# Reordering one core's attention and feed-forward kernel: value products, transposes, PSUM banks and the last tile

## The chip, the cores and the metric

The kernel runs on one core of a Trainium2 chip. The metric is the device time of one launch in microseconds (us). A core has TensorE (PE in the profile, with its weight loads as PEld), VectorE (DVE), ScalarE (ACT), GpSimd (POOL) and SyncE (SP). In this kernel POOL issues most of the loads.

## The reference, cut to what matters

```python
scores = q @ k.T / 8 + bias                   # 8 batches, 8 heads, 576 positions, head size 64
attn   = softmax(scores)
x      = (attn @ v).transpose(0, 2, 1, 3).reshape(4608, 512)
out    = ((x @ w_a) * (x @ w_b)) @ w_out      # 512 -> 1536 -> 512, bilinear, no activation
```

The kernel treats heads in pairs: 32 pairs, four for each batch. The 576 positions of a head are four tiles of 128 and a "tail" of 64.

## The kernel before

Step `s` computes the scores and exponentials of pair `s` and the value products of pair `s - 1`. Between them it puts **units**: pieces of the feed-forward part of earlier batches, four matmuls of 512 columns each. A unit is either `ff_a` (then a copy on ScalarE), `ff_b` (then a product on VectorE) or a third of an output tile.

The kernel takes eight banks of PSUM, the memory that matmuls write to, and its pools divide them so: `ps_sc` two buffers of two banks for scores, `ps_ff` two for the units ("ffn"), `ps_av` one and `ps_tr` one. From pair 12 on the units also take `ps_tr` at every third turn. The two pools with one bank:

```python
def t_k(p, where):                  # key transposes of pair p: four tiles, two tails
    ps = bank(where, BF16, f"trk{p}")
    for t in range(NM):
        nc.tensor.transpose(ps[:, 128 * t:128 * t + 128], blocks(kn, p)[:, t, :, :], ident)
    ...                             # c_k copies the bank to KT on VectorE, which frees it

def qk_tail(p):                     # scores with a tail; the last product has its own bank
    ...
    pt = bank(TR if p < R3 else AV, FP32, f"qktt{p}")      # R3 = 12

def norm(p, j0):                    # reciprocal of the sums and multiply, both read the bank
    ...

XD = set(range(11, NP - 1))         # pairs whose result is transposed by DMA, not on PE
```

One step, before the change. `A` are value products in bank `AV` (tiles 0 to 2) and in `TR` or, from step 12 on, `AV` (tiles 3 and 4). `N` is their normalisation, `U` a place for units, `e` says that pair `s + 1` is one of the first twelve:

```python
steps += [lambda: qk(s, 0), lambda: ex(s, 0), U, lambda: ex(s, 1), A(0, 1, 2), N(0), U,
          lambda: mul(s, 0), A(3, 4), N(3)]
if s - 1 in XD:
    steps += [lambda: t_x(s - 1), lambda: turns(s)]
steps += [U, lambda: mul(s, 1)]
if e:
    steps += [lambda: t_q(s + 1, TR), lambda: c_q(s + 1)]
steps += [lambda: qk(s, 2), lambda: ex(s, 2), U, lambda: ex(s, 3)]
if e:
    steps += [lambda: t_k(s + 1, TR), lambda: c_k(s + 1)]
steps += [U, lambda: mul(s, 2), U, lambda: mul(s, 3),
          lambda: qk_tail(s), lambda: ex_tail(s), U]
...
```

Steps 5 to 8 have fewer units than places (7, 6, 4 and 4), later steps have 9. The last output tile is computed in two halves of 256 columns, so that the first can be copied while the second is computed:

```python
def ff_last(c, tt):
    po = ff_bank(f"po{c}_{tt}")
    for x, cols in enumerate((slice(0, 256), slice(256, 512))):
        ...                                              # 12 matmuls into po[:, cols]
        copy(None if x else nc.scalar, ob[:, cols], po[:, cols])
        ...
```

The softmax here doesn't subtract the row's maximum and nothing guards it: scores larger than these inputs give would overflow.

## Time and profile before

| | kernel before |
|---|---|
| time | 425.61 us, median of 3 runs (425.33 to 426.5) |
| span of the profiled run | 423.3 us |
| PE / ACT / DVE busy | 97% / 58% / 47% |
| matmuls, and weight loads | 3420 each |

TensorE's share and its slices are shown in the prediction below, with the waits. Two rows of the page complete them: the granted TensorE clock and the busy share of the DMA engines, in tenths, in 40 slices of 10.6 us.

```profile
PEclk9999999999999999999999999999999999999999
DMA  9999999995929940999099908731021002002004
```

The clock is full nearly everywhere, so distances between matmuls can be compared nearly across the whole run. (Not so at the very start: up to 9.0 us fp32 transposes stand 213 ns apart and afterwards 109, which the first digit of the row doesn't show.) The DMA engines are full for the first nine slices, to about 95 us.

### The profile page before, as it was taken

To read this page: it belongs to the slowest core of one execution; us is meant where nothing else is said; L and a number is where in the kernel's file an instruction comes from. 1 tells how busy PE (TensorE), PEld (TensorE's weight loads), DVE (VectorE), ACT (ScalarE), POOL (GpSimd) and SP (SyncE) were. 2 spreads that over 40 slices of the span, in tenths; PEclk is the share of its full clock that TensorE was granted. 3 is DMA by queue.
4 is the path that set the end of the run, shared out by engine and by line. 5 is a ranking of instruction groups with operands and counts; after the bars stand their busy time and mean duration, and the time that the engine had idled before them with its cause. 6 is when DMAs were issued, how large, how long until landed. Compare 5 with 4: busy or idle time off the path is not lost.

```text
span 423.3 us, 8500 instructions
## 1 busy us (share of the span) xinstructions
PE 411.6 (97%) x3420; PEld 204.6 (48%) x3420; DVE 199.4 (47%) x491; ACT 243.9 (58%) x345; POOL 119.4 (28%) x161
## 2 busy tenths in 40 slices
PE   8899999999999999999999999999999999999995
PEld 3574555555444444444444444444444454444443
DVE  3775566555642565245535553355425650331420
ACT  4986566756656666576656665666556642322321
POOL 9999829704437000820083003000000000000000
PEclk9999999999999999999999999999999999999999
DMA  9999999995929940999099908731021002002004
GB/s 161 184 175 174 160 171 158 167 184 38 88 27 172 175 58 15 139 180 125 16 96 197 137 16 60 168 70 33 15 88 33 9 17 99 2 0 101 0 1 101
DMA packets 163017, 40.33 MB, mean 95 GB/s; under 512 B 153401, under 2 KB 158305, under 8 KB 162977
## 3 DMA queue, kind: packets, MB, share of 16 engines
q0 software_dynamic: 110448, 18.75, 60.3%
q1 hardware_dynamic: 51248, 20.59, 25.1%
q10 hardware_dynamic: 1280, 0.43, 0.5%
q8 instruction: 27, 0.44, 0.4%
q14 instruction: 14, 0.11, 0.1%
HBM read 38.77 MB, written 9.45 MB: 114 GB/s over the span
## 4 chain that ended last, share of the span: by engine, by line
PE 89%; DMA 5%; ACT 2%; DVE 1%; issue 1%; ACTq 0%; POOL 0%; DVEq 0%; POOLq 0%
PE pa L511 21%; PE pb L511 21%; PE po L542 21%; PE av L412 8%; PE qk L342 8%; DMA qn<-in_q_dram 3%; PE av L403 3%; PE qkt L367 2%; PE qkt L370 1%; ACT at L353 1%; DMA vm<-in_v_dram 1%; DMA k<-in_k_dram 1%; PE trx L475 1%; PE po L530 1%; DVE XG L449 1%
## 5 line engine op out<-in xcount | busy, mean ns | idle before, releaser
L353 ACT ACTIVATE at<-qk 128x1024 bf16<-128x1024 f32 x128 | 126.4, 1023 | 24.3 <-PE qk L342 24.1
L523 DVE TENSOR_TENSOR g<-pb,ha 128x512 bf16<-128x512 f32 x108 | 74.7, 692 | 118.0 <-PE pb L511 98.7
L511 PE MATMUL pa<-xn,wa 128*128 128x512 bf16 x432 | 111.2, 379 | 0.5 <-ACT ha L518 0.5
L511 PE MATMUL pb<-xn,wb 128*128 128x512 bf16 x432 | 111.2, 379 | 0.0
L518 ACT ACTIVATE ha<-pa 128x512 f32<-128x512 f32 x108 | 64.5, 598 | 69.8 <-PE pa L511 69.8
L542 PE MATMUL po<-wo,g 128*128 128x512 bf16 x420 | 100.2, 379 | 0.0
L361 DVE TENSOR_TENSOR at<-at,W 128x512 bf16<-128x512 bf16 (+1 forms) x128 | 60.1, 484 | 10.3 <-ACT at L353 8.8
L511 PEld LDWEIGHTS <-wa 128*128 128x128 bf16 x432 | 38.9, 98 | 48.5 <-issue 9.3
L511 PEld LDWEIGHTS <-wb 128*128 128x128 bf16 x432 | 38.9, 98 | 46.3 <-issue 6.6
L546 ACT ACTIVATE ob<-po 128x512 f32<-128x512 f32 x35 | 20.9, 597 | 67.9 <-PE po L542 67.9
L542 PEld LDWEIGHTS <-g 128*128 128x128 bf16 x420 | 37.2, 98 | 44.0 <-issue 7.4
L123 POOL DMA_DIRECT2D vm<-in_v_dram x32 | 28.2, 929 | 102.5 <-PE av L412 101.7
L412 PE MATMUL av<-vm,at 128*128 128x65 bf16 x992 | 43.3, 193 | 0.0
L412 PEld LDWEIGHTS <-at 128*128 128x128 bf16 x992 | 39.5, 97 | 3.9
L448 DVE RECIPROCAL rc<-av 128x6 f32<-128x6 f32 x64 | 12.1, 188 | 55.9 <-PE av L412 53.6
L403 PE MATMUL av<-vt,att 128*128 128x130 bf16 x156 | 34.9, 224 | 0.4
L381 ACT ACTIVATE att<-qkt 128x1024 bf16<-128x1024 f32 x32 | 32.6, 1020 | 0.0
L449 DVE TENSOR_TENSOR XG<-av,rc 128x384 bf16<-128x384 f32 x64 | 31.4, 491 | 2.2
L123 POOL DMA_DIRECT2D qn<-in_q_dram x28 | 24.4, 926 | 26.5 <-PE trq L291 19.1
L123 POOL DMA_DIRECT2D kn<-in_k_dram x28 | 24.5, 920 | 5.5 <-DMA vm<-in_v_dram 2.5
L342 PE MATMUL qk<-QTb,KTb 64*128 64x512 bf16 x160 | 24.2, 381 | 0.0
L403 PEld LDWEIGHTS <-att 128*128 128x128 bf16 x156 | 15.3, 98 | 15.3 <-DVE XG L449 10.7
(121 smaller groups left out, 247.0 us busy)
## 6 DMA issues: line engine op xcount, KB each, us to landing
out_dram<-ob SPq DMA_DIRECT2D x32, 256.0 KB, 3.8
vm<-in_v_dram POOLq DMA_DIRECT2D x28, 128.0 KB, 5.3
qn<-in_q_dram POOLq DMA_DIRECT2D x24, 128.0 KB, 8.4
kn<-in_k_dram POOLq DMA_DIRECT2D x24, 128.0 KB, 8.5
wa<-in_moe_w_a_dram POOLq DMA_DIRECT2D x3, 512.0 KB, 6.8
wb<-in_moe_w_b_dram POOLq DMA_DIRECT2D x3, 512.0 KB, 9.2
wo<-in_moe_w_out_dram POOLq DMA_DIRECT2D x1, 1536.0 KB, 13.4
W<-bias_tab POOLq DMA_DIRECT2D x4, 192.0 KB, 5.0
```

The source lines that it names most:

```text
L123: nc.gpsimd.dma_start(out=(vm[b % 2][:, h0:h1, t, 0:Dh] if dst is None else dst[b % 2][:, :].rearrange("p (t h d) -> p t h d", h=H, t=NM)[ ...
L342: nc.tensor.matmul(out=ps[:, hh, :], lhsT=kT_(p, t)[r, :], rhs=qT[r, :, :], start=True, stop=True)
L353: nc.scalar.activation(out=at[:, :, :], in_=ps[:, :, :], func=ACTF.Exp, scale=scale)
L361: nc.vector.tensor_tensor(out=at[:, :, lo:hi], in0=at[:, :, lo:hi], in1=w[:, :, y:(None if z < 0 else z):-1], op=MULT)
L381: nc.scalar.activation(out=at[:, 0:1024].rearrange("p (a x) -> p a x", a=2), in_=ps[:, :, :], func=ACTF.Exp, scale=scale)
L403: nc.tensor.matmul(out=pav[:, slot, :, :], lhsT=x, rhs=vt[b // 2 % 2][:, 4 * i + hp, :, 0:Dh + 1], start=fresh, stop=True, skip_group_chec ...
L412: nc.tensor.matmul(out=pav[:, slot, hh, :], lhsT=x, rhs=vm[i][:, 2 * hp + hh, t, 0:Dh + 1], start=False, stop=True, skip_group_check=True)
L449: nc.vector.tensor_tensor(out=xg[:, j0:j0 + n, :, :], in0=pav[:, 0:n, :, 0:Dh], in1=rc.unsqueeze(3).to_broadcast([128, n, 2, Dh]), op=MULT)
L511: nc.tensor.matmul(out=ff[key][:, :], lhsT=w[df // FW][:, mc, 128 * (df % FW):128 * (df % FW) + 128], rhs=xn_sb[mc][:, xin(c)], start=(i = ...
L518: nc.scalar.activation(out=ha[:, :], in_=ff["pa"][:, :], func=ACTF.Copy)
L523: nc.vector.tensor_tensor(out=g_sb[df][:, :], in0=ff["pb"][:, :], in1=ff["ha"][:, :], op=MULT)
L542: nc.tensor.matmul(out=po[:, :], lhsT=g_sb[df][:, 128 * tt:128 * tt + 128], rhs=wo_sb[:, df, :], start=(df == 0), stop=(df == NDF - 1))
```

## The change

Its intent is to close waits of TensorE for a PSUM bank, and to take a few transposes off it. The diff, cut to its core (left out: the DMA transposes of pair `s - 1` move along with the half in part 1):

```diff
-    warm_up(1)                                  # part 6
+    warm_up(3)
-    XD = set(range(11, NP - 1))                 # part 2
+    XD = set(range(8, NP - 1))
 def ff_last(c, tt):                             # part 5
-        po = ff_bank(f"po{c}_{tt}")
         for x, cols in enumerate((slice(0, 256), slice(256, 512))):
+            po = ff_bank(f"po{c}_{tt}_{x}")
@@ around step 4: part 4 (pair 4 behind the first two units)
-    t_k(4, FF)      # and c_k(4, ACT): now behind av_part(3, 3)
-    qk1(4, 0)
-    ex(4, 0)
-    qk1(4, 1)
-    ex(4, 1)
     norm(3, 0)
     norm(3, 3)
+    ff_mm(0, 0, wa_sb, "pa", 0, 3)
     t_x(3, AV, range(3))
-    ff_mm(0, 0, wa_sb, "pa", 0, 3)
-            steps += [U, U, lambda: qk1(4, 2), lambda: ex(4, 2), U, ...
+            steps += [U, U, lambda: qk1(4, 0), lambda: ex(4, 0), lambda: qk1(4, 1), U, lambda: ex(4, 1),
+                      lambda: qk1(4, 2), U, lambda: ex(4, 2), lambda: qk1(4, 3), lambda: ex(4, 3),
@@ steps 5 to 31
-                      lambda: mul(s, 0), A(3, 4), N(3)]
+                      lambda: mul(s, 0)]
+            av34 = [A(3, 4), N(3)]              # part 1: from step 12 on one unit later
+            if s < R3:
+                steps += av34
             steps += [U, lambda: mul(s, 1)]
+            if s >= R3:
+                steps += av34
+            steps += [lambda: qk(s, 2), lambda: ex(s, 2)]
             if e:                               # part 3: query transposes behind the scores,
                 steps += [lambda: t_q(s + 1, TR), lambda: c_q(s + 1)]
-            steps += [lambda: qk(s, 2), lambda: ex(s, 2), U, lambda: ex(s, 3)]
+            steps += [U, lambda: ex(s, 3), U, lambda: mul(s, 2)]
             if e:                               # key transposes one place later
                 steps += [lambda: t_k(s + 1, TR), lambda: c_k(s + 1)]
-            steps += [U, lambda: mul(s, 2), U, lambda: mul(s, 3),
-                      lambda: qk_tail(s), lambda: ex_tail(s), U]
+            steps += [U, lambda: mul(s, 3), lambda: qk_tail(s), lambda: ex_tail(s), U]
```

More of the change, by code (lines that the diff above doesn't have):

```diff
@@ L702 @@
     t_q(4, FF)
-    t_k(4, FF)
     c_q(4, ACT)
-    c_k(4, ACT)
     mul(3, 2)
@@ L712 @@
     av_part(3, 3)
-    qk1(4, 0)
-    ex(4, 0)
-    qk1(4, 1)
-    ex(4, 1)
+    t_k(4, FF)
+    c_k(4, ACT)
     norm(3, 0)
     norm(3, 3)
+    ff_mm(0, 0, wa_sb, "pa", 0, 3)
     t_x(3, AV, range(3))
-    ff_mm(0, 0, wa_sb, "pa", 0, 3)
     t_x(3, AV, range(3, 5))
@@ L750 @@
         if s == 4:
-            steps += [U, U, lambda: qk1(4, 2), lambda: ex(4, 2), U, lambda: qk1(4, 3), lambda: ex(4, 3),
+            steps += [U, U, lambda: qk1(4, 0), lambda: ex(4, 0), lambda: qk1(4, 1), U, lambda: ex(4, 1),
+                      lambda: qk1(4, 2), U, lambda: ex(4, 2), lambda: qk1(4, 3), lambda: ex(4, 3),
                       lambda: mul(4, 0), U, tails4, U, lambda: qk_tail(4), lambda: ex_tail(4),
@@ L758 @@
             steps += [lambda: qk(s, 0), lambda: ex(s, 0), U, lambda: ex(s, 1), A(0, 1, 2), N(0), U,
-                      lambda: mul(s, 0), A(3, 4), N(3)]
+                      lambda: mul(s, 0)]
+            av34 = [A(3, 4), N(3)]
             if s - 1 in XD:
-                steps += [lambda: t_x(s - 1), lambda: turns(s)]
+                av34 += [lambda: t_x(s - 1), lambda: turns(s)]
+            if s < R3:
+                steps += av34
             steps += [U, lambda: mul(s, 1)]
+            if s >= R3:
+                steps += av34
+            steps += [lambda: qk(s, 2), lambda: ex(s, 2)]
             if e:
                 steps += [lambda: t_q(s + 1, TR), lambda: c_q(s + 1)]
-            steps += [lambda: qk(s, 2), lambda: ex(s, 2), U, lambda: ex(s, 3)]
+            steps += [U, lambda: ex(s, 3), U, lambda: mul(s, 2)]
             if e:
                 steps += [lambda: t_k(s + 1, TR), lambda: c_k(s + 1)]
-            steps += [U, lambda: mul(s, 2), U, lambda: mul(s, 3),
-                      lambda: qk_tail(s), lambda: ex_tail(s), U]
+            steps += [U, lambda: mul(s, 3), lambda: qk_tail(s), lambda: ex_tail(s), U]
             if s - 1 not in XD:
```

## The prediction

> **What bounds the kernel now.** I read the page first, then who waited for whom on TensorE, then the matmuls in order of time, and last the start and the tail of the chain that ended last.
>
> ```profile
> PE 411.6 (97%) x3420; PEld 204.6 (48%) x3420; DVE 199.4 (47%) x491; ACT 243.9 (58%) x345; POOL 119.4 (28%) x161
> PE   8899999999999999999999999999999999999995
> ACT  4986566756656666576656665666556642322321
> ```
>
> TensorE (PE) is busy in every slice after the first three, while ScalarE (ACT) is near its limit only at the start. So a change pays only if it takes matmuls off PE or closes a gap between them. "97% busy" hides such gaps, because a matmul's record (379 ns for 512 columns) is longer than its distance to the next one: four in a row take 0.86 us, about 216 ns each. I therefore read distances from start to start.
>
> ```profile
> PE trq L291 <- DVE XG L449: 2.0, 4, 0.7
> PE po L530 <- ACT ob L255: 0.5, 1, 0.5
> PEld L403 <- DVE XG L449: 10.7, 21, 0.5
> ...
> 175.72 1.04 PE L542 MATMUL po<-wo,g 128*128 128x512 bf16 x4
> 176.59 0.22 PE L403 MATMUL av<-vt,att 128*128 128x130 bf16 x1
> ...
> 177.50 1.03 PE L542 MATMUL po<-wo,g 128*128 128x512 bf16 x4
> 178.54 0.23 PE L403 MATMUL av<-vt,att 128*128 128x130 bf16 x1
> ```
>
> The first two lines are PE waits and the third is a wait of the weight load (PEld), 21 times. The timeline shows what those 21 cost. Four feed-forward matmuls take 0.87 us up to the next product at 175.72, but 1.04 us at 177.50, before the second half of the value products: normalisation (L449) has not yet freed their only PSUM bank. Over the trace's starts this excess is 181 to 188 ns, 21 times, once for each pair from 12 on.
>
> **What the Trainium skill says.** "Perfetto Trace Analysis", section "Optimizing Tensor Performance", says that independent groups should rotate through PSUM banks so that evacuation overlaps the next matmuls; the waits above are the price of one bank used twice in a row, so the trace agrees. "TensorE: Matmul & The Clock Gate", Part 1, gives N/2.4 GHz + 2.5 ns from start to start on the warm clock and about 3.4 us of sustained work before the clock is warm, at a moment that varies from run to run. The trace agrees: 216 ns for 512 columns, fp32 transposes 0.21 us apart at 5.9 to 7.5 us and 0.12 us apart at 9.1 us, and the full clock granted from 9.0 us. "TensorEngine Tiling (Array Packing)", section "Key Properties", says that changing the tiling mode drains the engine; here a score matmul of 64 rows costs 98 ns extra on entry and 95 on leaving, and the change keeps the number of such switches.
>
> **Part 1, second half of the value products one unit later.** For steps 12 to 31 one more unit (4 matmuls, 0.86 us) stands between the two halves. Normalisation ends some 1.05 us after the first half (reciprocal 0.2 us, multiply 0.56, hand-overs), so 1.72 us cover it. The last of the 21 waits is in step 32, which isn't changed. Gain 20 x 0.185 = **3.7 us**. The new neighbours, scores right behind value products, pay the same 99 ns that they pay now behind a unit.
>
> **Part 2, pairs 8 to 10 transposed by DMA.** 3 x 5 transposes leave PE: 15 x 56 ns = **0.85 us**; those five in a row take 0.28 us now. The replacements need 3.7 us to land (median of 40 in the table of DMA issues) and their reader is chunk 2, some ten microseconds later: hidden.
>
> **Part 3, transposes of the early pairs spaced apart.** Steps 5 to 10 now begin the query transposes one unit behind the second half, in a bank that normalisation still reads.
>
> ```profile
> 59.98 0.40 PE L412 MATMUL av<-vm,att 128*128 128x65 bf16 x8
> 60.42 0.18 DVE L448 RECIPROCAL rc<-av 128x4 f32<-128x4 f32 x1 [0.35 <-PE av L412]
> 60.64 0.42 DVE L449 TENSOR_TENSOR XG<-av,rc 128x256 bf16<-128x256 f32 x1
> 61.13 0.40 PE L291 MATMUL trq<-cst_sb,qn 128*128 128x128 bf16 x4 [0.74 <-DVE XG L449]
> ```
>
> The excesses from start to start are 0.53, 0.91, 0.55, 0.47 and 0.80 us: 3.26 us in five steps (step 9 has none). The change puts the scores of two tiles ahead, 0.54 us plus a switch, 0.64 us: left are 0.26 and 0.15 us, so 2.85 us are won. But it also moves the key transposes one unit later, and in steps 6, 7 and 8, which have fewer units than places for them, nothing stands between these and the tail scores, whose last product takes the same bank:
>
> ```profile
> 71.90 0.38 PE L311 MATMUL trk<-cst_sb,kn 128*128 128x128 bf16 x4
> 72.43 0.56 DVE L257 COPY KT<-trk 128x768 bf16<-128x768 bf16 x1 [0.59 <-PE trk L303]
> 73.10 0.39 PE L367 MATMUL qkt<-KT 128*128 128x128 bf16 x4
> 73.54 0.22 PE L373 MATMUL qktt<-KT 128*128 128x64 bf16 x2
> ```
>
> The copy ends 1.09 us after the transposes begin. Today a unit lies between; without it the last product would be reached at 0.33 + 0.44 us, so it waits 0.38 us, three times: 1.15 us back. With some 0.15 us for other neighbours the net gain is **1.55 us**. Built, the changed order shows exactly these neighbours in these three steps.
>
> **Part 4, pair 4 behind the first two units.** Around 28 to 35 us PE loses 0.53 us (key transposes behind a copy on ACT), 0.45 and 0.33 (transposes behind normalisation) and 0.63 (second unit behind the copy of the first). The move fills most of these; I work out that unit 2 starts at 34.2 instead of 34.84. But the four exponentials of 1.02 us, of which two now run before 33.7 us, all come after the first copy. From 33.45 us ACT then has 4 x 1.02 + 4 copies x 0.60 + 1.25 for the tails = 7.7 us, with small gaps to 41.7, and unit 8 (at 41.64 now) can't start before its fourth copy. The 0.6 us won are given back: net **0**, between -0.4 and +0.6.
>
> **Part 5, last tile in two banks.** The second half no longer waits for the copy of the first; the gap is 637 ns from start to start (0.5 in the list). Nothing follows but the last half's copy and transfer, unchanged: **0.64 us**.
>
> **Part 6, two more warm-up matmuls.** They fill the wait for the first keys (4.83 to 5.69 us at 0.427 each), and may make the clock warm one window earlier. But
>
> ```profile
> 6.26 1.27 SPq L145 DMA_DIRECT2D kt<-in_k_dram  x2
> 11.29 0.30 PE L618 MATMUL trt<-id,kt 128*128 128x128 f32 x1
> DMA to landing us min/median/max: 4.0/4.1/4.2
> ```
>
> The second tail-key load is issued at 6.9 and lands 4.2 us later, at 11.1; the transposes at 11.29 follow it at once, and pair 1's first scores stand behind them. Even if everything earlier moves up 0.9 us, these don't: **0.1 us**.
>
> **Sum.** 3.7 + 0.85 + 1.55 + 0 + 0.64 + 0.1 = 6.84 us. 425.61 - 6.84 = 418.8; I shade it to 418.6, since Part 4 and Part 6 can miss upwards more easily than downwards. That is 1.6% less.
>
> **Rivals.** (a) The second half's move only shifts the wait: normalisation of it comes later, and the tail score product that takes this bank next finds it busy. Against it: two units and the scores still lie between, 2.3 us against the 1.05 needed. It would give back up to 3.7 us: 422. (b) ACT becomes the bound. It has 6 us of work in each 10 of the middle, so not there; only in Part 4's ten microseconds. (c) Everything gained at the start counts: if the warm clock comes at 5.7 us and the key tails land earlier, Part 6 is worth up to 0.9 us, and Part 4 its 0.6: 417.2. (d) The DMA transposes and the turned keys share one queue, so one of them late would hold chunk 2. Chunk 2 begins in step 13, three steps after the earliest of them; a miss would cost a few us once. I give it 5%.
>
> **Range and chances.** Parts 1, 2 and 5, 5.2 us, are measured gaps or matmuls and nearly certain: 420.4 without the rest. Part 3 may end between 0.8 and 2.6, Part 4 and Part 6 between -0.4 and +1.5 together. So 416.8 to 420.8. Two per cent below 425.61 is 417.1, reached only if nearly every doubt falls well: 13%. Slower would need a stall that I don't see: 1%.
>
> **What would show it.** PE matmuls fall by 13 to 3407. The wait of L403's weight loads on L449 falls from 21 to about 1, and the distance before the second value half to 0.87. Query transposes after step 4 wait at most 0.3 us. A new wait "qktt behind KT's copy" of about 0.4 us appears three times near 62, 70 and 78 us. Unit 8 starts within 0.4 us of 41.6. The first tail transposes stay near 11.3 us. No wait at the last tile. I would be wrong if PE waits anew in the middle (rival a), or if the early part moves as a whole by a microsecond or more.

## The result, and the profile after

| | before | after |
|---|---|---|
| time, 4 runs each | 425.47 us (425.02 to 426.5) | 418.69 us (418.46 to 419.84) |
| ratio | | 0.9843, 95% interval 0.9817 to 0.9868 |
| span of the profiled run | 423.3 us | 416.6 us |

A ratio here is the mean time of one kernel's fast runs over that of the other's of the same rounds, so it is not quite the ratio of the two medians.

From the page of the kernel after, the engines' busy time and the slices of PE and ACT:

```profile
PE 403.1 (97%) x3350; PEld 207.2 (50%) x3407; DVE 197.5 (47%) x485; ACT 245.3 (59%) x345; POOL 119.3 (29%) x161
PE   8799999999999999999999999999999999999996
ACT  4887565766656766677666665666567642322321
```

The weight loads are 13 fewer, 3407: 15 transposes less, two warm-up matmuls more. The 3350 matmuls are no contradiction, since 57 matmul records are missing from this trace; I count by the weight loads and measure by starts. PE's share is still 97%: the share says nothing about the 6.7 us that went, because the span shrank with them.

The waits of PE after the change, with the line waited in, what was waited for, us in total, times and the longest:

```profile
PE trt L618 <- DMA kt<-in_k_dram: 1.1, 1, 1.1
PE qktt L373 <- DVE KT L257: 1.0, 4, 0.4
...
PE trq L291 <- DVE XG L449: 0.2, 1, 0.2
```

The query transposes' wait for normalisation fell from 2.0 us to 0.2. The second line is new: the tail product waits for the key copy. The list gives it four times; by start-to-start distances it is there five times, as shown below. The wait of L403's weight loads for normalisation, 21 times before, is there once, in step 32, which the change leaves alone. The timeline of PE, a middle step, in us from the span's start and us of duration:

```profile
174.83 1.67 PE L542 MATMUL po<-wo,g 128*128 128x512 bf16 x7
176.34 0.22 PE L403 MATMUL av<-vt,att 128*128 128x130 bf16 x1
```

Seven records stand for eight matmuls (one is missing). The second half of the value products follows them at once. Before, the same product stood 1.04 us behind four matmuls that take 0.87.

To see where the time came from, I cut both traces at a landmark, the start of each pair's first value product with tail values (L403), and compare the stretches:

| stretch | before, us | after, us | difference |
|---|---|---|---|
| start to pair 2 | 25.37 | 25.51 | +0.14 |
| pair 2 to pair 4 (part 4) | 21.79 | 21.28 | -0.51 |
| pair 4 to pair 11 (parts 2 and 3) | 73.17 | 71.61 | -1.56 |
| pair 11 to pair 31 (part 1) | 223.59 | 219.73 | -3.86 |
| pair 31 to the last matmul's start (part 5) | 75.09 | 74.46 | -0.63 |
| from there to the end | 4.31 | 4.06 | -0.25 |

The sum is -6.7 us, which is the difference of the spans (-6.68). The first stretch varies with the loads from run to run (25.3 to 26.4 us over the runs below), so variants are compared by the later stretches as well as by the ratio.

### The profile page after: what moved, and what is told of

Same layout as the page of the kernel before. It is cut to its first block, busy times and chain, and to the rows that moved or that the text cites. A ratio compares the mean times of both kernels' runs of the same rounds, so it can differ in the third digit from the quotient of the medians.

```text
span 416.6 us, 8424 instructions
## 1 busy us (share of the span) xinstructions
PE 403.1 (97%) x3350; PEld 207.2 (50%) x3407; DVE 197.5 (47%) x485; ACT 245.3 (59%) x345; POOL 119.3 (29%) x161
## 4 chain that ended last, share of the span: by engine, by line
PE 90%; DVE 3%; DMA 2%; POOL 2%; issue 2%; ACT 0%; POOLq 0%; DVEq 0%; ACTq 0%
PE pa L511 22%; PE pb L511 22%; PE po L542 21%; PE av L412 9%; PE qk L342 7%; PE av L403 2%; PE qkt L367 1%; DMA kn<-in_k_dram 1%; PE qkt L370 1%; DMA W<-bias_tab 1%; PE qktt L373 1%; PE po L530 1%; PE trx L475 1%; DVE KT L257 1%; DVE XG L449 1%
## 5 line engine op out<-in xcount | busy, mean ns | idle before, releaser
L511 PE MATMUL pb<-xn,wb 128*128 128x512 bf16 x411 | 109.1, 379 | 1.1 <-issue 0.2
L542 PE MATMUL po<-wo,g 128*128 128x512 bf16 x403 | 96.3, 379 | 1.1 <-issue 0.3
L361 DVE TENSOR_TENSOR at<-at,W 128x512 bf16<-128x512 bf16 (+1 forms) x128 | 59.1, 483 | 7.4 <-ACT at L353 5.5
L403 PE MATMUL av<-vt,att 128*128 128x130 bf16 x156 | 34.7, 222 | 0.0
L403 PEld LDWEIGHTS <-att 128*128 128x128 bf16 x156 | 15.3, 98 | 7.4 <-issue 0.7
## 6 DMA issues: line engine op xcount, KB each, us to landing
wo<-in_moe_w_out_dram POOLq DMA_DIRECT2D x1, 1536.0 KB, 13.1
```

The source lines that it names most:

```text
L361: nc.vector.tensor_tensor(out=at[:, :, lo:hi], in0=at[:, :, lo:hi], in1=w[:, :, y:(None if z < 0 else z):-1], op=MULT)
L403: nc.tensor.matmul(out=pav[:, slot, :, :], lhsT=x, rhs=vt[b // 2 % 2][:, 4 * i + hp, :, 0:Dh + 1], start=fresh, stop=True, skip_group_chec ...
L511: nc.tensor.matmul(out=ff[key][:, :], lhsT=w[df // FW][:, mc, 128 * (df % FW):128 * (df % FW) + 128], rhs=xn_sb[mc][:, xin(c)], start=(i = ...
L542: nc.tensor.matmul(out=po[:, :], lhsT=g_sb[df][:, 128 * tt:128 * tt + 128], rhs=wo_sb[:, df, :], start=(df == 0), stop=(df == NDF - 1))
```

## The experiments

Every edit is against the changed kernel. First each part was undone alone, then causes were taken away. Kernels of one group shared one chip and the same runs of the kernel before. Four runs each; the ratio is against the kernel before. All outputs are right.

| kernel | median, us | ratio, 95% interval | before, us |
|---|---|---|---|
| u1_half_back | 422.60 | 0.9933 [0.9915, 0.9952] | 425.74 |
| u2_pe_transposes | 419.48 | 0.9855 [0.9841, 0.9870] | 425.74 |
| u3_banks_back | 420.00 | 0.9863 [0.9849, 0.9878] | 425.74 |
| u4_pair4_back | 419.03 | 0.9847 [0.9830, 0.9863] | 425.74 |
| u5_last_one_bank | 419.19 | 0.9851 [0.9822, 0.9880] | 425.86 |
| u6_one_warm_up | 418.90 | 0.9830 [0.9813, 0.9846] | 425.86 |
| n1_tail_in_av | 417.40 | 0.9792 [0.9772, 0.9812] | 425.86 |
| n2_copy_first | 418.19 | 0.9819 [0.9798, 0.9839] | 425.86 |
| n3_tail_keys_on_act | 418.83 | 0.9840 [0.9825, 0.9854] | 425.64 |
| n5_pair8_first | 416.73 | 0.9794 [0.9780, 0.9809] | 425.64 |
| n6_all_four | 417.31 | 0.9802 [0.9785, 0.9818] | 425.64 |

An interval is about 0.2% to each side, 0.8 us. Parts worth half a microsecond can't be read from these ratios; for them I read the stretch of the trace in which the part lies, and the rest of the trace as a control.

**u1_half_back: part 1 undone.**

```diff
-            if s < R3:
-                steps += av34
+            steps += av34
             steps += [U, lambda: mul(s, 1)]
-            if s >= R3:
-                steps += av34
```

> The changed kernel (418.69 us) with part 1 alone undone: the second half of the value products of steps 12 to 31 back in its old place, one unit after the first half. Theory (one bank used twice in a row): the 0.19 us before the second half come back in each of 20 steps, and nothing else; 3.9 us, so about 422.5, and the distance between the first halves of neighbouring steps goes from 11.06 back to 11.25 us. Rival a (the move only shifted part of the wait, the rest being hidden elsewhere): less than 3 us come back.

The stretch from pair 11 to pair 31 is 223.59 us again, to the hundredth that of the kernel before, so part 1 is worth **3.86 us**. The weight loads' wait is back as it was:

```profile
PEld L403 <- DVE XG L449: 10.7, 21, 0.5
```

This disposes of the rival that the wait merely moves: a pair takes 10.99 us on average instead of 11.18 (each stretch over 20 pairs), and no other wait of that size appears in the stretch.

**u2_pe_transposes: part 2 undone.**

```diff
-    XD = set(range(8, NP - 1))
+    XD = set(range(11, NP - 1))
```

> The changed kernel with part 2 alone undone: pairs 8 to 10 transposed on PE again. Theory: 15 transposes of 56 ns, 0.84 us, come back, 419.5. Rival: in steps 9 to 11 they share a bank with key transposes and tail products, so their copies bring waits of their own and more than 1.2 us come back.

From pair 8 to pair 11 it takes 35.62 us instead of 35.05: part 2 is worth **0.57 us**. The transposes themselves stand there with 0.28 us each time, as before. The rest shows in the changed kernel, where two units now follow each other directly:

```profile
92.04 1.03 PE L511 MATMUL pa<-xn,wa 128*128 128x512 bf16 x4
93.06 1.02 PE L511 MATMUL pb<-xn,wb 128*128 128x512 bf16 x4
```

From start to start that is 1.02 us for four matmuls, where 0.86 is undisturbed. It happens three times (near 92.7, 104.5 and 115.7 us), 0.15 us each: the next unit needs one of two feed-forward banks, and the product on VectorE (or copy on ScalarE) that frees it isn't done. With the transposes back on PE the distance at the first of these places is 0.86. So the transposes had been standing in a short wait, and only part of their time comes free. Against that, one wait of 0.17 us for normalisation that the variant has is missing in the change.

**u3_banks_back: part 3 undone.** The transposes are put back in their old places of the step.

> The changed kernel with part 3 alone undone: query and key transposes of steps 5 to 10 back in their old places. From the two traces steps 5 to 11 gained 1.56 us together, 0.84 of them by part 2, so theory (the wait of the query transposes was traded for a wait of the last tail product behind the keys' copy, in five steps and not in three): 0.7 us come back, 419.4; five waits of qktt of 0.31 to 0.38 us go, five waits of trq of 0.5 to 0.9 us return. As predicted before (three new waits): 1.55 us come back, 420.2.

From pair 4 to pair 11 it takes 72.40 us. The changed kernel takes 71.61, of which 0.23 is a wait for a load in step 7 (below) that this variant doesn't have; four other runs (u1, u4, u6 and n3), whose edits leave these steps alone and which have no such wait, take 71.38. So part 3 is worth **1.02 us**. The old wait is back, nearly whole:

```profile
PE trq L291 <- DVE XG L449: 1.7, 4, 0.7
```

**u4_pair4_back: part 4 undone.** Pair 4's key transposes, first scores and exponentials stand in front of the first two units again.

> The changed kernel with part 4 alone undone: key transposes and the first two score tiles of pair 4 ahead of the first units again. Theory from the traces (ScalarE's records overlap, its exponentials start 0.92 to 0.95 us apart and not 1.02, so it isn't the bound at unit 8): 0.5 us come back, 419.2, unit 8 starts 0.5 us later than 41.27. As predicted (ScalarE takes it all back): 0, unit 8 at 41.3.

From pair 2 to pair 4 it takes 21.78 us instead of 21.28; in all the other variants it takes 21.27 or 21.28. So part 4 is worth **0.50 us**. The total can't show this: the ratio differs from the change's by 0.04% only, less than either interval, and in the profiled run the front had a wait of its own of 0.5 us for a key load, up to 20.7 us.

Why ScalarE doesn't take the gain back is read in its timeline in the changed kernel:

```profile
33.44 0.60 ACT L518 ACTIVATE ha<-pa 128x512 f32<-128x512 f32 x1 [1.73 <-PE pa L511]
33.98 1.02 ACT L353 ACTIVATE at<-qk 128x1024 bf16<-128x1024 f32 x1
...
35.65 2.85 ACT L353 ACTIVATE at<-qk 128x1024 bf16<-128x1024 f32 x3
38.36 0.63 ACT L518 ACTIVATE ha<-pa 128x512 f32<-128x512 f32 x1
39.59 0.22 ACT L380 ACTIVATE att<-qktt 128x64 bf16<-128x64 f32 x1 [0.60 <-PE qktt L373]
...
40.62 0.60 ACT L518 ACTIVATE ha<-pa 128x512 f32<-128x512 f32 x1
```

The first copy begins at 33.44 and the next activation at 33.98, 0.54 us later, though the copy's record is 0.60 us long. Three exponentials of 1.02 us take 2.85 us, so they begin 0.92 us apart. Records on ScalarE overlap by some 0.06 to 0.10 us, and in this stretch it was even idle for 0.60 us, waiting for TensorE. The fourth copy ends at 41.22. The records from the first copy to the fourth add up to some 7.75 us and the idle times to 0.76, but the stretch takes 7.78: overlap gives back 0.7 us. "Perfetto Trace Analysis", section "DVE / Act Engine Instruction (TENSOR_ADD, Activation, etc)", says why in the Trainium skill's terms: a record runs to the acknowledgement of the write, but the next instruction may begin to fetch when the execution is done. This trace agrees, with the 0.92 us against 1.02.

**u5_last_one_bank: part 5 undone.**

```diff
+        po = ff_bank(f"po{c}_{tt}")
         for x, cols in enumerate((slice(0, 256), slice(256, 512))):
-            po = ff_bank(f"po{c}_{tt}_{x}")
```

> The changed kernel with part 5 alone undone: both halves of the last tile in one bank. Theory: the second half waits for the copy of the first again, 0.64 us, 419.3. Rival: the transfer of the first half lands later than that of the second would, so only part of it, under 0.3 us, shows in the time.

The timelines of PE at the end, first of the changed kernel, then of this variant:

```profile
410.07 2.78 PE L530 MATMUL po<-wo,g 128*128 128x256 bf16 x24
```

```profile
412.12 1.47 PE L530 MATMUL po<-wo,g 128*128 128x256 bf16 x12 [0.47 <-ACT ob L255]
```

All 24 matmuls run through in one group in the first; in the second the last twelve wait for the copy of the first half. The last stretch is 0.64 us longer: part 5 is worth **0.64 us**.

**u6_one_warm_up: part 6 undone** (`warm_up(1)`).

> The changed kernel with part 6 alone undone: one warm-up matmul and not three behind the table. Theory: the warm clock comes at 9 us and not near 5.9 us, the first scores start 0.4 us later, but the first tail transposes stay at 11.3 to 11.5 us because they wait for the second load of tail keys, and the time stays at 418.7 within 0.2. Rival c: what is won at the start counts, and 0.4 to 0.9 us come back.

The ratio of 0.9830 is no worse than that of the change. In eleven runs with three warm-up matmuls the full clock came between 4.75 and 9.90 us; with one, at 8.99 (the kernel before) and at 10.64 (this run). (These are the traces' own clock records; the distance between fp32 transposes falls from 213 to 109 ns there.) The first tail transposes began between 11.14 and 11.64 us in all with three but n3 and n6, which load their keys differently. In seven of these nine they began 0.13 or 0.14 us after the last load of these keys had landed, so they waited for it:

```profile
11.43 0.30 PE L618 MATMUL trt<-id,kt 128*128 128x128 f32 x1 [1.12 <-DMA kt<-in_k_dram]
```

That line is from the changed kernel, whose clock was full from 4.75 us on; it reached this place early and waited 1.12 us. In the other two, u4 and n2, the clock was full only from 9.76 and 9.90 us, and the keys had landed 0.55 and 0.31 us before. There TensorE itself was late, as the timeline of u4 shows, with no wait between the scores and the transposes:

```profile
11.15 0.39 PE L342 MATMUL qk<-QT,KT 64*128 64x512 bf16 x2
11.47 0.33 PE L618 MATMUL trt<-id,kt 128*128 128x128 f32 x1
```

In this variant, with the clock at 10.64, they started at 11.96, 0.98 us after the keys. So the keys set this start only when the clock comes early enough. Part 6 is worth **nothing that these runs can measure**. Whether it guards against a late clock, one run can't tell.

**n1_tail_in_av: the new wait taken away.** The last tail product gets the other single bank, which is free at that moment:

```diff
-        pt = bank(TR if p < R3 else AV, FP32, f"qktt{p}")
+        pt = bank(TR if p < 5 else AV, FP32, f"qktt{p}")
```

> New: the changed kernel with the last tail product of pairs 5 to 11 in the bank of the value products, as pairs 12 and on have it, so that it no longer waits for the copy of the next pair's keys. Theory: five waits of 0.31 to 0.38 us (1.75 us in steps 5 to 9) go and nothing replaces them: 417.0, steps 5 to 11 gain 3.3 us over the kernel before and not 1.56. Rival: the bank of the value products makes the next step's first half wait for ScalarE to read the tail, or ScalarE's order holds it: under 0.9 us gained.

This run is faster than the change: 417.40 us. All the waits of the tail product are gone, in steps 5 to 9. In the changed kernel they measure 0.31, 0.37, 0.37, 0.37 and 0.31 us from start to start, 1.74 us together. But its trace won only 0.58 us from pair 4 to pair 11, for now step 7 waits 0.89 us and step 5 waits 0.46 us for key loads. That led to n5.

**n2_copy_first: why steps 5 and 9 wait too.** There a unit does stand between the key transposes and the tail scores. The timeline of VectorE and PE in step 5 of the changed kernel:

```profile
52.02 0.69 DVE L523 TENSOR_TENSOR g<-pb,ha 128x512 bf16<-128x512 f32 x1 [0.51 <-PE pb L511]
52.63 0.55 DVE L361 TENSOR_TENSOR at<-at,W 128x768 bf16<-128x768 bf16 x1
53.10 0.55 DVE L257 COPY KT<-trk 128x768 bf16<-128x768 bf16 x1
53.70 0.22 PE L373 MATMUL qktt<-KT 128*128 128x64 bf16 x2 [0.36 <-DVE KT L257]
```

The transposes began at 51.75 us, but VectorE runs a unit's product and a multiplication by the bias table ahead of the copy. The edit puts the transposes and the copy ahead of that multiplication, `mul(s, 2)`.

> The changed kernel with the copy of the next pair's keys on VectorE ahead of the multiplication of tile 2 and not behind it; the order on TensorE is the same. Theory: in steps 5 and 9, where a unit stands between transposes and tail products, the copy was late only because it stood behind that multiplication (0.55 us), so these two waits (0.36 and 0.31) go; steps 6, 7 and 8 keep 0.3 to 0.4 us each, since there nothing stands between. Sum 0.5 to 0.9 us, about 418.0. Rival (the bank's chain is just longer than one unit): no wait goes.

The waits of steps 5 and 9 are gone, and the stretches of pair 4 to 5 and 8 to 9 are each 0.30 us shorter; the three of steps 6 to 8 stay, 0.37 us each. So VectorE's order is the cause in two of the five. The total gained little (418.19), since step 7 waited for keys in this run, 1.28 us by the distances from start to start. In the timeline of PE the records name the loads twice:

```profile
71.94 0.23 PE L311 MATMUL trk<-cst_sb,kn 128*128 128x128 bf16 x1 [0.34 <-DMA kn<-in_k_dram]
...
72.77 0.23 PE L311 MATMUL trk<-cst_sb,kn 128*128 128x128 bf16 x1 [0.59 <-DMA kn<-in_k_dram]
```

**n3_tail_keys_on_act: a miss.** The tail keys of the first pairs are issued by ScalarE instead of SyncE, to land sooner.

```diff
-    load_pad(nc.sync, k, kt32, 0, 1)
+    load_pad(nc.scalar, k, kt32, 0, 1)
```

> The changed kernel with the first load of tail keys issued from ScalarE's queue, some 3 us earlier than behind the other loads on SyncE's. Theory (the first tail transposes wait for this load, so the warm-up could win nothing): they start near 10.3 and not 11.4 us, and the value products of pair 0 up to 1 us earlier. What is left at the end depends on the loads of the next batches: in steps 5 and 7 the key transposes reach the landing of their last block (it held them 0.2 to 0.9 us in the runs so far), so theory 2 (these loads are a second limit up to 72 us): under 0.4 us of it is left at step 8, 418.4 or more. Rival (PE alone sets the pace there): all of it is left, 417.7.

No gain: 418.83 us. The transposes do begin sooner, at 10.83 us, but the second of them waits for the query tail until 11.52. And ScalarE, busy with issuing, loads its table later:

```profile
3.81 1.28 ACT L220 ACT_TABLE_LOAD   x1 [3.81 <-issue]
14.84 1.70 DVE L361 TENSOR_TENSOR at<-at,W 128x512 bf16<-128x512 bf16 x4 [2.01 <-DMA W<-bias_tab]
```

In the changed kernel the table load begins at 2.35 us, and the multiplication by the bias table `W` at 14.12. Here the bias table is written 0.6 us later (issued at 5.51 us instead of 4.90), the multiplication begins at 14.84, and pair 0's value products begin at 17.34 us instead of 16.87. That the edit itself delays them is not shown: the first load of `W` is issued at 9.46 us here and at 9.44 in the change, and in u3, without this edit, the multiplication began later still, at 14.93. What the traces do show is why earlier tail keys win nothing. In all 13 traces pair 0's value products begin at least 2.49 us after that first multiplication, and in seven, this one among them, 2.49 or 2.50 us after it. There the bias table sets their start, and not the tail keys.

**n5_pair8_first: the keys of pair 8.** Their loads are the ones that step 7 waits for. In the changed kernel POOL issues the loads of batch 2 here (start, duration, what is loaded, idle time before):

```profile
49.16 1.02 POOL L163 DMA_DIRECT2D wo<-in_moe_w_out_dram  x1
...
62.84 0.89 POOL L123 DMA_DIRECT2D qn<-in_q_dram  x1 [7.29 <-PE trk L311]
63.76 3.50 POOL L123 DMA_DIRECT2D kn<-in_k_dram  x4
```

The page names a TensorE instruction as what POOL waited for, but that one had long been done: the 7.3 us end when the output weights, issued at 49.16 and 13.1 to 13.4 us on the way, have landed. With them, eight loads had been issued up to this point. The semaphores in the trace give the reason: POOL's loads report their landing on eight semaphores in turn (numbers 111 to 118), and the held load waits for number 111, on which the output weights report. So the program as it was built sets this limit. The four key loads come last, each for all heads, so pair 8's keys are complete only with the fourth. The edit issues pair 8's queries and keys ahead of the others', on top of n1's edit:

```diff
-    load_t(q, qn, 2, 0, 8)
-    load_t(k, kn, 2, 0, 8)
+    load_p(q, qn, 2, 0)
+    load_p(k, kn, 2, 0)
+    load_t(q, qn, 2, 2, 8)
+    load_t(k, kn, 2, 2, 8)
```

> The changed kernel with the last tail product of pairs 5 to 11 in the value products' bank (as n1_tail_in_av, 417.4) and the queries and keys of pair 8 loaded ahead of those of pairs 9 to 11. Theory: the key transposes of step 7 no longer wait for the landing of the last block of batch 2 (0.55 us in n1's trace), so step 7 gains 0.4 us like its neighbours, and 416.8 to 417.0 come out. Rival: the loads behind are delayed and pairs 9 to 11 or the output weights wait: 417.4 or more.

POOL is held in the same way, at the ninth load again, and its timeline now names the output weights:

```profile
62.92 0.75 POOL L129 DMA_DIRECT2D kn<-in_k_dram  x1 [7.56 <-DMA wo<-in_moe_w_out_dram]
```

But the keys of pair 8 are there in time, no load is waited for in steps 5 to 9, and the stretch from pair 4 to pair 11 takes 69.66 us. That is 1.72 us less than the 71.38 of a clean run of the change, about the 1.74 us of the five waits. At **416.73 us** (416.66 to 417.32) it beats both kernels: 2.1% below the kernel before, by an interval that reaches from 1.9 to 2.2%. Its profiled run, the slowest of the four, had a 0.7 us wait for values at the front besides.

Not all of the difference to n1's trace (71.03 us in this stretch) is the edit's doing. Step 7's 0.89 us is: pair 8's keys landed at 66.91 us, in the changed kernel at 71.66. Step 5's 0.46 us was a wait for pair 6's keys, whose loads the edit leaves alone; n5's trace reached that step 0.89 us later than n1's. And by the ratios, 0.9794 and 0.9792, n5 and n1 can't be told apart.

**n6_all_four: n5 with n2 and n3 on top.**

> Changes of n5_pair8_first, n2_copy_first and n3_tail_keys_on_act together. Theory: no tail product waits, step 7 doesn't wait for its loads; only the keys of pair 6 in step 5 may still wait for theirs. 416.3 to 416.9, over 2% below the kernel before. Rival: with the tail product in another bank the order of the copies doesn't matter, and the early part is given back at step 5: no better than n5_pair8_first.

At 417.31 us it is no better than n5; the intervals overlap. With n1's bank the waits that n2 removes are gone already, and n3's edit again wins nothing at the front, where the first multiplication by the bias table began at 14.80 us.

## Why the prediction was right or wrong

The time, 418.69 us, is next to the predicted 418.6. The sum is this close partly by luck: two of its terms were off by half a microsecond in opposite directions.

| term | predicted, us | measured, us | from |
|---|---|---|---|
| part 1 | 3.7 | 3.86 | u1 |
| part 2 | 0.85 | 0.57 | u2 |
| part 3 | 1.55 | 1.02 | u3 |
| part 4 | 0 | 0.50 | u4 |
| part 5 | 0.64 | 0.64 | u5 |
| part 6 | 0.1 | none seen | u6 |
| load wait in step 7 | not foreseen | -0.23 | trace |
| front, and the end | not foreseen | -0.14, +0.25 | traces |

The measured terms add up to 6.47 us of the 6.68. The 0.2 us left lie between pairs 9 and 10, where parts 2 and 3 touch the same waits: there part 2 saves 0.49 us with part 3 undone (the kernel before against u3), but 0.31 us with it (u2 against the change).

- **Part 1** held as worked out: twenty waits closed (0.193 us each, 0.185 predicted), the one in step 32 stays. The rival (a), a shifted wait, fell with u1.
- **Part 2** failed in the sentence "3 x 5 transposes leave PE: 15 x 56 ns". They do leave, but at three places what stood behind them then waits 0.15 us for a feed-forward bank.
- **Part 3** failed in "in steps 6, 7 and 8 ... nothing stands between". The mechanism and its size were right (0.38 us predicted, 0.37 measured), but it happens five times, not three: 1.74 us instead of 1.15. In steps 5 and 9 a unit stands between, and I took that as enough; n2 shows that VectorE's two instructions ahead of the copy use the unit up. I had looked at TensorE's order alone.
- **Part 4** failed in "From 33.45 us ACT then has 4 x 1.02 + 4 copies x 0.60 + 1.25 for the tails = 7.7 us, with small gaps to 41.7". Unit 2 did start at 34.09, near the 34.2 worked out, but I added record lengths, and ScalarE's records overlap. The fourth copy ended at 41.22 and unit 8 started at 41.27 (41.64 before), still at the heels of that copy. Half of rival (c), part 4's gain counting, came true; 0.50 us lies inside the range given for the part.
- **Part 5** held to the hundredth.
- **Part 6** was right for this trace: the tail transposes waited for their keys and began at 11.43 us. It is not a rule for every run, since in u4, n2 and u6 a late clock set their start.
- Rival (b), ScalarE as a bound, was not seen even in part 4's ten microseconds: unit 8 does wait some 0.15 us for the fourth copy, but equally in the kernel before, in the change and in u4 (1.02 us from unit 7's start instead of 0.86). Rival (d), a late DMA transpose, did not come, but I looked for late transfers in the wrong place: it is the plain loads up to some 72 us that an earlier TensorE runs into.

## What to carry to other kernels

When a transpose is moved closer to the reader of its bank, count what the engine that empties the bank has queued ahead of the copy, not only what TensorE has in between. Measure an engine's capacity by the distance from start to start, also for ScalarE: adding record lengths makes a bound where there is none. And a gain that lets TensorE run ahead is only worth what the next load allows; here the bank for the tail product won 0.35 us over a clean run of the change (71.38 us) in n1's trace, where key loads were late, and 1.72 us in n5's, where none was.

## What the Trainium skill lacked or had wrong

- "Perfetto Trace Analysis", section "Identifying the Most-Contended Engine", calls the occupancy of Vector, Scalar and GpSimd a fair measure of how close they are to their limit. It gives no size for how far that is off. Here ScalarE's exponentials with records of 1.02 us begin 0.92 us apart when they stand back to back, so adding record lengths, as the prediction did, overstates their cost by about 10%.
- "TensorE: Matmul & The Clock Gate", Part 1, puts the full clock around 4 us into sustained matmuls and lets it vary by 500 ns to each side from run to run (further on it warns that one kernel had 6, 11 or 14 slow matmuls). In eleven runs with the same warm-up it lay anywhere between 4.75 and 9.90 us, which is 3.55 to 8.7 us after the first matmul at 1.20 us.
- "TensorEngine Tiling (Array Packing)", section "Key Properties", says that a change of the tiling mode drains the engine, but gives no size. Here it was 96 ns on entry and 93 on leaving (312 and 308 ns from start to start instead of 216; the prediction read 98 and 95).
- No page that I found says when POOL is held by loads still under way. Here the ninth load waited 7.3 us, until the load issued eight before it had landed; with other loads in between (n5) it was again the ninth, and 7.6 us. In both traces the two loads share one of eight landing semaphores, so this is the program's limit; whether the chip has one of its own, no run here shows.
